# A block-causal attention and gMLP kernel on one core: from an order kept for TensorE alone to one order for every engine

## The chip, the cores and the metric

The kernel runs on one core of one Trainium2 chip. The metric is the device time of one execution in microseconds (us); before the change the median of three runs is 747.5 us (747.38 to 748.92). Five engines work side by side, each through its own list of instructions in a fixed order: PE (TensorE: matmuls, with weight loads as PEld), DVE (VectorE), ACT (ScalarE), POOL (GpSimd) and SP (SyncE, which here only issues DMAs). An instruction waits at the head of its engine's list until the semaphores it needs have been raised.

## What is computed

```python
# q, k, v: (8, 8, 576, 64); block = 64
scores = scale * np.matmul(q, k.transpose(0, 1, 3, 2))
scores = np.where(block_i >= block_j, scores, -1e9)
attn = softmax(scores)                      # max, exp, sum, divide
x = np.matmul(attn, v)  -> (8, 576, 512)    # heads side by side
h = np.maximum(x @ w_in, 0.0)               # 512 -> 1024
u, v = h[..., :512], h[..., 512:]
v_n = (v - mean(v)) / np.sqrt(var(v) + 1e-6)
v_s = np.einsum('ts,bsd->btd', w_spatial, v_n) + b_spatial[None, :, None]
out = (u * v_s) @ w_out                     # 512 -> 512
```

The large matmuls of the second half are done in float32r, each operand split into a high part and a rest (hi, lo), three products for one.

## The kernel before

A batch has 8 heads, worked as four **pairs** (pr 0 to 3) of two heads. Batch 0 has a start of its own, in which scores are transposed on TensorE and the weights are split in the background. From batch 1 on, a loop takes one pair after another (32 pairs in all, 28 of them in this loop), and into each pair's attention it weaves a quarter of the gMLP of the batch before.

For one pair, in the source's order:

- `scores_8`: the last 64 rows of both heads (tile **p8**, 128 x 576): two matmuls into two PSUM banks, a DVE pass that scales, masks and takes the row maximum (L476), Exp on ACT with the row sums (L483), sum and reciprocal on DVE (L491, L494), the scaling of p8 by the reciprocal on POOL (L497).
- one gMLP group, if the loop's credit allows (`group`).
- `scores_run`: the eight matmuls of the other rows into six banks, **p3** first (512 columns, one tile for each head), then p2, then p1 with p0; for each the same DVE pass, Exp, sum, scaling.
- `av_pair` of the pair *before*: the products with V into two banks, then `x_evac`: ACT casts the bank into x (L395), DVE subtracts for the rest (L396).
- `turn_blocks`: DVE transposes p in 32 x 32 blocks into the buffer pb (L556 to L558 for p8, L563 and L565 for the others), and `regroup` moves pb into ptt by eight DMAs (L574), for the next pair's `av_pair`. Three calls of these stand behind each gMLP group.

Six PSUM banks are used in a ring, ten to a pair: the first bank of `av_pair` is the one from which DVE reads the first head's p3, the second that of the second head's p3. Two more banks, ps_m, go round among the gMLP groups. A group's matmuls start when what was two groups earlier has been read out of its bank.

The groups of a batch's gMLP: v groups (mv; five, of 128 rows and the **tail** of 64), u groups (mu; eight), spatial groups (ms; eight), output groups (mo; eight). A v group has four stages: matmuls and read-out into vr (L623; for the tail L634, L635, L636); statistics (L640, L641); the reciprocal root by Ln and Exp on ACT (L643, L644) with four small DVE steps (L645 to L657); normalising and splitting on ACT (L662, L668) and POOL (L669). Stage 1 is emitted with the group, and each later group that is emitted moves all groups behind it one stage on (`issue`). An ms group is read out by a multiplication on DVE (u, L720), then cast (gh, L723) and subtracted (gl, L724). Its matmuls need all four full v groups' splits (vh, vl) and the tail's.

What sets the order: `mm` chains every matmul of the loop to the one before it, so PE follows the source. On DVE, ACT, POOL and SP a compile-time scheduler with a model of its own sets the order; it is free to put a ready instruction ahead of one that stands earlier in the source. At run time every engine's list is fixed.

Of the kernel before, what the change touches and what calls it, by code (L numbers as in the profile page):

```python
# [55 lines left out]
def kernel(  # L56
# [171 lines left out]
    last = [None]  # L228

    def mm(out, lhsT, rhs, start, stop):  # L230
        ins = nc.tensor.matmul(out, lhsT, rhs, start=start, stop=stop).ins  # L231
        if last[0] is not None:
            tc.add_manual_dep(
                ins, last[0].name,
                mybir.DependencyInfo(mybir.DependencyClass.NoSync, mybir.DependencyReason.DATA),
                reason="order",
            )
            last[0] = ins
        elif ordered:
            last[0] = ins  # L240

    ordered = []
# [32 lines left out]
    def scores(b, pr, i):  # L275
# [8 lines left out]
        if hd < 2:  # L284
# [5 lines left out]
            mm(ps[:, :n], raw[js, qs], raw[js, :n], True, True)  # L290
# [5 lines left out]
        else:  # L296
            n = S
            for z in range(2):
# [3 lines left out]
                mm(ps[:, :HT], raw[:, Q8:], raw[:, zs], True, True)  # L302
# [166 lines left out]
    def soft(st, t, hd, p, parts):  # L469
# [17 lines left out]
    def normalise(st, tiles):  # L487
# [13 lines left out]
    def scores_8(b, pr):  # L501
        raw = raws[(b, pr)]
        st = stats[(b, pr)] = st_p.tile([P, 32], F32, tag="sst", name=f"sst_{b}_{pr}", bufs=3)
        parts = []
        for z in range(2):
            ps = bank(f"s8_{b}_{pr}_{z}")
            mm(ps[:, :HT], raw[:, Q8:], raw[:, z * HT:(z + 1) * HT], True, True)
            parts.append(ps[:, :HT])
        soft(st, 8, 0, p8[:, :S], parts)
        normalise(st, [(8, 0, p8[:, :S])])  # L510

    def scores_run(b, pr):

# [3 lines left out]
        for t in (3, 2, 1, 0):  # L517
            for hd in range(2):
# [59 lines left out]
    def av_pair(b, pr):  # L578
        ptt = ptts.pop((b, pr))
        vt = vts.pop((b, pr))  # L580
        for z in range(2):
            av = bank(f"av_{b}_{pr}_{z}")
            to = av[:, :HT].rearrange("p (a q) -> p a q", a=2)
            for c in range(5):
                for j in range(2):
# [4 lines left out]
                        ptt[:, 2 * z:2 * z + 2, at:at + C_N[c]], c == 0, c == 4,  # L590
                    )
            x_evac(b, pr, av[:, :HT], lambda x, z=z: x[:, z * HT:(z + 1) * HT], HT)
        tail_evac(b, pr)


    def moe(b):
# [155 lines left out]
        order = "vuvuvuvuvuuuu" if b else "v" * 5 + "u" * 8  # L752
# [73 lines left out]
    ordered.append(True)  # L826
    queue = moe(0)
    credit = 0.0

    behind = []  # L830

    def issue(f):
# [6 lines left out]
        behind.append(gen)  # L839

    def group():
        nonlocal credit
        if queue and credit > 0.0:
            t, f = queue.pop(0)
            credit -= t
            issue(f)
            return True
        return False

    for g in range(NPAIR, len(pairs)):  # L850
        b, pr = pairs[g]
        credit += G_PAIR
        rest = []
        for hd in range(2):
            for t in (3, 2, 1, 0):
                rest.append(lambda t=t, hd=hd: turn_blocks(b, pr, t, hd))
            rest.append(lambda hd=hd: regroup(b, pr, hd))
        rest.insert(0, lambda: turn_blocks(b, pr, 8, 0))
# [92 lines left out]
```

## Time and profile before

| what | value |
|---|---|
| median of 3 runs | 747.5 us (747.38 to 748.92) |
| the profiled execution: its time, its span | 749.12 us, 747.3 us |
| granted TensorE clock, mean | 0.993 |
| busy in the span: PE, PEld, DVE, ACT, POOL | 93%, 78%, 62%, 51%, 37% |
| PE waiting for DVE's u (L720) before mo, in all | 19.9 us |
| ACT and POOL waiting for what DVE gives (the longest three kinds) | 107.4, 101.5 and 50.1 us |

From batch 2 on the profile repeats itself every 87.3 us, six times; PE is busy for 81.8 us of each. Names: s are score matmuls, p probabilities, sst their sums and maxima, av the products with V, mv, mu, ms, mo the gMLP's banks, vr and st a v group and its statistics. A row of the timeline has the start (us), the duration, engine, line, operation, output and inputs, partitions x elements, a count, and in brackets the idle time just before with the one who ended it.

### The profile page before, as it was taken

What the parts mean: (1) busy time and instruction counts of PE and PEld (TensorE: products, weight loads), DVE (VectorE), ACT (ScalarE), POOL (GpSimd) and SP (SyncE); (2) the same over time, 40 slices, a digit from 0 to 9 for tenths busy, and PEclk for the clock granted to TensorE, in tenths of its full rate; (3) what the DMA queues carried; (4) which work ended last, traced back from release to release, by engine and by line L of the source; (5) the groups of instructions that cost most, each with busy time, mean ns of one, the idle gap of its engine ahead of it and who ended that gap; (6) DMA issues with size and microseconds to landing.
All of it is one profiled execution on the core that took longest, in us unless ns stands there. A gap on an engine that the chain in (4) does not pass through costs nothing.

```text
span 747.3 us, 14409 instructions
## 1 busy us (share of the span) xinstructions
PE 691.7 (93%) x4864; PEld 583.6 (78%) x4864; DVE 464.9 (62%) x1755; ACT 383.8 (51%) x1088; POOL 276.4 (37%) x428
## 2 busy tenths in 40 slices
PE   9999787999999999999999999999999999999998
PEld 6545576977888877887788778888778877888897
DVE  5985686466666675557864666666755578543521
ACT  5866654545544564446644455444644466442532
POOL 4775455232434224233342324342242334422121
PEclk9999899999999999999999999999999999999999
DMA  6444553664544634656246645446346562344001
GB/s 211 145 142 143 150 142 107 159 178 96 140 111 129 186 102 100 168 149 163 68 124 156 174 103 139 107 130 177 106 103 172 142 170 65 94 121 120 1 16 48
DMA packets 53660, 94.42 MB, mean 126 GB/s; under 512 B 5970, under 2 KB 43346, under 8 KB 53588
## 3 DMA queue, kind: packets, MB, share of 16 engines
q1 hardware_dynamic: 53588, 93.52, 46.5%
q8 instruction: 38, 0.62, 0.3%
q14 instruction: 34, 0.28, 0.1%
HBM read 38.18 MB, written 9.44 MB: 64 GB/s over the span
## 4 chain that ended last, share of the span: by engine, by line
DVE 39%; PE 25%; ACT 16%; POOL 8%; issue 6%; DMA 3%; SPq 3%; POOLq 0%; DVEq 0%; ACTq 0%
PE mo L231 12%; DVE pb L563 9%; DVE p L476 8%; ACT p L483 7%; PE ms L231 6%; POOL p L497 4%; DVE st L640 3%; PE s L231 3%; ACT vr L662 3%; SPq L574 2%; DVE pb L556 2%; POOL vl L669 2%; PE mv L231 2%; DVE sst L491 1%; DVE vr L636 1%
## 5 line engine op out<-in xcount | busy, mean ns | idle before, releaser
L497 POOL TENSOR_SCALAR p<-p,sst 128x384 f32<-128x384 f32 (+4 forms) x252 | 136.2, 557 | 203.3 <-DVE sst L494 101.5
L483 ACT ACTIVATE p<-p,sst 128x384 f32<-128x384 f32 (+4 forms) x252 | 145.0, 577 | 47.6 <-DVE sst L476 44.6
L476 DVE CUSTOM_DVE_ANT_0 p<-s,mask 128x384 f32<-128x384 f32 (+4 forms) x252 | 113.9, 470 | 38.8 <-PE s L231 38.4
L231 PE MATMUL s<-raw 64*128 64x256 f32 (+4 forms) x640 | 127.6, 446 | 2.3 <-DVE nmax L291 1.8
L231 PE MATMUL mu<-x,wi_hi 128*128 128x288 f32 x512 | 113.2, 300 | 8.9 <-ACT u L694 8.9
L231 PEld LDWEIGHTS s<-raw 64*128 64x128 f32 (+1 forms) x640 | 73.6, 191 | 41.0 <-issue 23.3
L231 PE MATMUL mv<-wi_hi,x 128*128 128x512 f32 x256 | 90.2, 414 | 12.5 <-DVE vr L635 9.9
L563 DVE STREAM_TRANSPOSE pb<-p 128x384 f32<-128x384 f32 (+2 forms) x224 | 96.2, 452 | 5.6 <-POOL p L497 4.4
L231 PEld LDWEIGHTS mu<-x,wi_hi 128*128 128x128 f32 x512 | 85.4, 188 | 12.6 <-ACT u L694 10.5
L720 DVE TENSOR_TENSOR u<-ms,u 128x288 f32<-128x288 f32 x64 | 28.2, 441 | 100.3 <-PE ms L231 100.2
L231 PE MATMUL av<-ptt,v 128*64 128x32 f32 (+4 forms) x1120 | 86.8, 306 | 2.3 <-DVE sst L476 2.1
L231 PEld LDWEIGHTS av<-ptt,v 128*64 128x64 f32 x1120 | 77.0, 137 | 13.5 <-DVE sst L476 4.6
L723 ACT CAST gh<-u 128x288 fp32r<-128x288 f32 x64 | 27.6, 432 | 113.2 <-DVE u L720 107.4
L231 PE MATMUL ms<-ws_hi,vh 128*128 128x288 f32 x256 | 80.8, 316 | 3.6 <-ACT u L694 3.5
L669 POOL TENSOR_TENSOR vl<-vr,vh 128x512 fp32r<-128x512 f32 x32 | 41.2, 1288 | 102.8 <-ACT vh L668 102.7
L231 PE MATMUL ms<-ws_hi,vl 128*128 128x288 f32 x256 | 76.2, 298 | 1.0 <-POOL vl L669 0.3
L724 POOL TENSOR_TENSOR gl<-u,gh 128x288 fp32r<-128x288 f32 x48 | 38.4, 801 | 100.5 <-ACT gh L723 100.5
L231 PE MATMUL mo<-gh,wo_hi 128*128 128x288 f32 x256 | 56.9, 303 | 19.9 <-DVE u L720 19.9
L231 PE MATMUL ms<-ws_lo,vh 128*128 128x288 f32 x256 | 75.3, 294 | 0.0
L231 PEld LDWEIGHTS mv<-wi_hi,x 128*128 128x128 f32 x256 | 49.2, 192 | 28.6 <-DVE vr L635 11.9
L231 PE MATMUL mu<-x,wi_lo 128*128 128x288 f32 x256 | 69.8, 295 | 0.0
L745 ACT COPY o<-mo 128x288 f32<-128x288 f32 x64 | 25.5, 399 | 70.9 <-PE mo L231 62.6
(121 smaller groups left out, 1296.0 us busy)
## 6 DMA issues: line engine op xcount, KB each, us to landing
ptt<-pb SPq DMA_DIRECT2D x224, 200.0 KB, 4.0
raw<-qk SPq DMA_DIRECT2D x31, 608.0 KB, 3.8
v<-v SPq DMA_DIRECT2D x32, 320.0 KB, 3.0
outT<-o SPq DMA_DIRECT2D x64, 144.0 KB, 3.3
rwi<-w_in SPq DMA_DIRECT2D x8, 512.0 KB, 3.5
rwo<-w_out SPq DMA_DIRECT2D x4, 512.0 KB, 4.2
rws<-w_spT SPq DMA_DIRECT2D x4, 288.0 KB, 2.7
rwt<-w_spT SPq DMA_DIRECT2D x2, 144.0 KB, 4.8
```

The lines of the kernel that those rows point to most:

```text
L231: ins = nc.tensor.matmul(out, lhsT, rhs, start=start, stop=stop).ins
L476: nc.vector.tensor_tensor_reduce(out=p[:, at:at + n], in0=ps, in1=mk, scale=-0.125, scalar=BIG if m == 0 else st[:, k:k + 1], op0=ALU.add, ...
L483: nc.scalar.activation(p, p, AF.Exp, bias=mx, scale=-1.0, accum_out=st[:, 10 + k:11 + k])
L497: nc.gpsimd.tensor_scalar(out=p, in0=p, scalar1=st[:, k:k + 1], scalar2=1.0, op0=ALU.mult, op1=ALU.mult)
L563: nc.vector.transpose(to(hd * XH + 32 * t, [[P, m], *dims] if m > 1 else dims), p[:, :m * P])
L640: nc.vector.bn_stats(out=st[:m, 0:6], in_=vr[:m, :])
L662: nc.scalar.activation(vr[:m, :], vr[:m, :], AF.Identity, bias=st[:m, 13:14], scale=st[:m, 12:13])
L669: nc.gpsimd.tensor_tensor(out=vl, in0=vr, in1=vh.bitcast(F32), op=ALU.subtract)
L720: nc.vector.tensor_tensor(out=uz, in0=ps[:, :HT], in1=uz, op=ALU.mult)
L723: nc.scalar.copy(gh[:, dc, :], uz)
L724: (nc.vector if dc == ND - 1 else nc.gpsimd).tensor_tensor(out=gl[:, dc, :], in0=uz, in1=gh[:, dc, :].bitcast(F32), op=ALU.subtract)
L745: nc.scalar.copy(o, ps[:, :HT])
```

## The change

1. `mm` becomes a plain matmul. A new function `in_order` chains every instruction traced since its last call to the one before it *on the same engine*, for PE, DVE, ACT, POOL and SP. From batch 1's first pair on (batches counted from 0) all engines follow the source. `pass_over` leaves out what `step_background` emits: weight preparation, still in the scheduler's hands.
2. The source's order is written anew. p8's transposes stand right behind its scaling in `scores_8`. In `scores_run` the sum and reciprocal of a pair of tiles stand behind the DVE passes of the next pair of tiles, and p3's first transposes before the last of these. `av_pair` yields after each half, and transposes stand between the read-outs; one gMLP group stands behind the first head's p2, the others behind the last transposes.
3. The buffer vr has three places in place of two.
4. Batch 0's gMLP starts v v v u v u v u ..., with the tail third, in place of five v groups and then eight u groups.

No instruction is added or removed; PE's order is the same but for batch 0's gMLP.

```diff
-        f = ff_p.tile([P, 512], F32, tag="vr", name=f"f{name}", bufs=2)[:, :n]
+        f = ff_p.tile([P, 512], F32, tag="vr", name=f"f{name}", bufs=3)[:, :n]
...
+    def in_order():
+
+        new = traced.instructions[seen[0]:]
+        seen[0] += len(new)
+        for i in new:
+            if i.engine in last:
+                tc.add_manual_dep(
+                    i, last[i.engine].name,
...
+                )
+            last[i.engine] = i
+
+    mm = nc.tensor.matmul
...
-        soft(st, 8, 0, p8[:, :S], parts)
-        normalise(st, [(8, 0, p8[:, :S])])
+        top(st, 8, 0, p8[:, :S], parts)
+        norm(st, [(8, 0, p8[:, :S])])
+        turn_blocks(b, pr, 8, 0)
...
-            normalise(st, tiles)
+            if due:
+                norm(st, due)
+            due = tiles
+        turn_blocks(b, pr, 3, 0)
+        norm(st, due)
...
-            vr = ff_p.tile([P, DH], F32, tag="vr", name=f"vr_{b}_{c}", bufs=2)
+            vr = ff_p.tile([P, DH], F32, tag="vr", name=f"vr_{b}_{c}", bufs=3)
...
-        order = "vuvuvuvuvuuuu" if b else "v" * 5 + "u" * 8
+        order = "vuvuvuvuvuuuu" if b else "vvvuvuvuuuuuu"
...
         scores_8(b, pr)
+        in_order()
         group()
         scores_run(b, pr)
-        if g > NPAIR:
-            av_pair(*pairs[g - 1])
-            if pr == 0:
-                queue += moe(b - 1)
-        n = max(n, g * NT)
+        av = av_pair(*pairs[g - 1]) if g > NPAIR else iter([])
+        next(av, None)
+        turn_blocks(b, pr, 3, 1)
+        next(av, None)
+        next(av, None)
+        turn_blocks(b, pr, 2, 0)
+        in_order()
+        if g > NPAIR and pr == 0:
+            queue += moe(b - 1)
+        group()
+        turn_blocks(b, pr, 1, 0)
+        turn_blocks(b, pr, 0, 0)
+        regroup(b, pr, 0)
+        turn_blocks(b, pr, 2, 1)
+        turn_blocks(b, pr, 1, 1)
+        turn_blocks(b, pr, 0, 1)
+        regroup(b, pr, 1)
+        in_order()
         while group():
-            step_background(n)
-            n += 1
-            for f in rest[:3]:
-                f()
-            del rest[:3]
-        for f in rest:
-            f()
+            pass
```

How this moves instructions is shown at three places of batch 3, which stand for batches 2 to 7. The names carry batch, pair, head and a serial number; rows with `128x1` behind an `ISA` row are that pass's read-out of the maxima.

**DVE at pair 0, from p8's passes on; before:**

```order
L476 ISA p8_96,sst_3_0_2867<-s8_3_0_1_2870,mask_98,sst_3_0_2867 128x288
L476 ISA sst_3_0_2867 128x1
L476 ISA p3_3_0_0_2892,sst_3_0_2867<-s3_3_0_0_2878,mask_98 128x512
L476 ISA sst_3_0_2867 128x1
L491 TENSOR_SCALAR sst_3_0_2867<-sst_3_0_2867 128x1
L494 RECIPROCAL sst_3_0_2867<-sst_3_0_2867 128x1
L476 ISA p3_3_0_1_2895,sst_3_0_2867<-s3_3_0_1_2880,mask_98 128x512
L476 ISA sst_3_0_2867 128x1
L476 ISA p2_3_0_0_2902,sst_3_0_2867<-s2_3_0_0_2882,mask_98 128x384
L476 ISA sst_3_0_2867 128x1
L556 STREAM_TRANSPOSE pb_3_0_2972<-p8_96 128x3x8x16
```

**and in the changed kernel:**

```order
L484 ISA p8_96,sst_3_0_2867<-s8_3_0_1_2870,mask_98,sst_3_0_2867 128x288
L484 ISA sst_3_0_2867 128x1
L499 TENSOR_SCALAR sst_3_0_2867<-sst_3_0_2867 128x1
L502 RECIPROCAL sst_3_0_2867<-sst_3_0_2867 128x1
L574 STREAM_TRANSPOSE pb_3_0_2878<-p8_96 128x3x8x16
L575 STREAM_TRANSPOSE pb_3_0_2878<-p8_96 128x8x16
L576 STREAM_TRANSPOSE pb_3_0_2878<-p8_96 128x8x16
L484 ISA p3_3_0_0_2896,sst_3_0_2867<-s3_3_0_0_2882,mask_98 128x512
```

The first p3 pass, which frees `av_pair`'s first bank, stood right behind p8's passes; now it stands behind p8's sum, reciprocal and all three p8 transposes, and the first of these waits for POOL's scaling.

**ACT from the tail's read-out (mv_2_4) to p8's Exp of pair 1; before:**

```order
L662 ACTIVATE vr_2_1_3004<-vr_2_1_3004,st_2_1_3005 128x512
L634 COPY vr_2_4_3056<-mv_2_4_3055 64x512
L668 CAST vh_2_1_3090<-vr_2_1_3004 128x512
L694 ACTIVATE u_2_2992<-mu_2_0_2_3075 128x288
L643 ACTIVATE st_2_4_3057<-st_2_4_3057,eps_113 64x1
L644 ACTIVATE st_2_4_3057<-st_2_4_3057 64x1
L662 ACTIVATE vr_2_4_3056<-vr_2_4_3056,st_2_4_3057 64x512
L623 ACTIVATE vr_2_2_3097<-mv_2_2_3096 128x512
L675 CAST vs_a_123<-vr_2_4_3056 64x512
L483 ACTIVATE p8_96,sst_3_1_3122<-p8_96,sst_3_1_3122 128x576
```

**and in the changed kernel:**

```order
L655 COPY vr_2_4_3056<-mv_2_4_3055 64x512
L664 ACTIVATE st_2_1_3014<-st_2_1_3014,eps_113 128x1
L665 ACTIVATE st_2_1_3014<-st_2_1_3014 128x1
L715 ACTIVATE u_2_3008<-mu_2_0_2_3075 128x288
L683 ACTIVATE vr_2_1_3013<-vr_2_1_3013,st_2_1_3014 128x512
L689 CAST vh_2_1_3090<-vr_2_1_3013 128x512
L644 ACTIVATE vr_2_2_3097<-mv_2_2_3096 128x512
L664 ACTIVATE st_2_4_3057<-st_2_4_3057,eps_113 64x1
L665 ACTIVATE st_2_4_3057<-st_2_4_3057 64x1
L491 ACTIVATE p8_96,sst_3_1_3122<-p8_96,sst_3_1_3122 128x576
```

The tail's Ln and Exp (st_2_4), for which DVE's small steps wait, stood ahead of the next v group's read-out (vr_2_2); now they stand behind v group 1's normalising and cast and behind that read-out.

**ACT from the last v group's Exp (st_2_3) to the first gh; before:**

```order
L694 ACTIVATE u_2_2992<-mu_2_1_0_3261 128x288
L644 ACTIVATE st_2_3_3234<-st_2_3_3234 128x1
L662 ACTIVATE vr_2_3_3233<-vr_2_3_3233,st_2_3_3234 128x512
L694 ACTIVATE u_2_2992<-mu_2_1_1_3289 128x288
L668 CAST vh_2_3_3328<-vr_2_3_3233 128x512
L694 ACTIVATE u_2_2992<-mu_2_1_2_3313 128x288
```

**and in the changed kernel:**

```order
L715 ACTIVATE u_2_3008<-mu_2_1_1_3298 128x288
L664 ACTIVATE st_2_3_3243<-st_2_3_3243,eps_113 128x1
L665 ACTIVATE st_2_3_3243<-st_2_3_3243 128x1
L715 ACTIVATE u_2_3008<-mu_2_1_2_3318 128x288
L683 ACTIVATE vr_2_3_3242<-vr_2_3_3242,st_2_3_3243 128x512
L689 CAST vh_2_3_3333<-vr_2_3_3242 128x512
```

The last v group's normalising and cast stood ahead of the read-out of the last u group before the ms groups (mu_2_1_2); now they stand behind it.

More of the change, by code (lines that the diff above doesn't have):

```diff
@@ L225, in load_pair, with pass_over @@
         raws[(b, pr)] = raw
[L228 to L242, printed above, removed]
+    traced = nc.cur_bb.bb
+    last = {}
+    seen = [0]
+    def pass_over():
+        seen[0] = len(traced.instructions)
+    def in_order():
[5 more added lines that the diff above has]
+                    i, last[i.engine].name,
+                    mybir.DependencyInfo(
+                        mybir.DependencyClass.NoSync, mybir.DependencyReason.DATA
+                    ),
+                    reason="order",
+                )
+            last[i.engine] = i
+    mm = nc.tensor.matmul
     vts = {}
@@ L289, in scores @@
             raw = raws[(b, pr)]
-            mm(ps[:, :n], raw[js, qs], raw[js, :n], True, True)
+            mm(ps[:, :n], raw[js, qs], raw[js, :n], start=True, stop=True)
             nc.vector.tensor_tensor_reduce(
@@ L301, in scores @@
                 raw = raws[(b, pr)]
-                mm(ps[:, :HT], raw[:, Q8:], raw[:, zs], True, True)
+                mm(ps[:, :HT], raw[:, Q8:], raw[:, zs], start=True, stop=True)
                 nc.vector.tensor_tensor_reduce(
@@ L467, with top @@
              (1, 0): 4, (0, 0): 5, (1, 1): 6, (0, 1): 7, (8, 0): 8}
-    def soft(st, t, hd, p, parts):
+    def top(st, t, hd, p, parts):
         k = PLACE[(t, hd)]
@@ L485, in soft, with norm @@
         )
-    def normalise(st, tiles):
+    def norm(st, tiles):
         k0 = PLACE[tiles[0][:2]]
@@ L506, in scores_8 @@
             ps = bank(f"s8_{b}_{pr}_{z}")
-            mm(ps[:, :HT], raw[:, Q8:], raw[:, z * HT:(z + 1) * HT], True, True)
+            mm(ps[:, :HT], raw[:, Q8:], raw[:, z * HT:(z + 1) * HT], start=True, stop=True)
             parts.append(ps[:, :HT])
-        soft(st, 8, 0, p8[:, :S], parts)
-        normalise(st, [(8, 0, p8[:, :S])])
+        top(st, 8, 0, p8[:, :S], parts)
+        norm(st, [(8, 0, p8[:, :S])])
+        turn_blocks(b, pr, 8, 0)
     def scores_run(b, pr):
@@ L525, in scores_run @@
                         ps[(0, hd)] = bk[:, n:n + P]
-                mm(ps[(t, hd)], raw[js, S + t * P:S + (t + 1) * P], raw[js, :n], True, True)
+                mm(
+                    ps[(t, hd)], raw[js, S + t * P:S + (t + 1) * P], raw[js, :n],
+                    start=True, stop=True,
+                )
+        due = None
         for ts in ((3,), (2,), (1, 0)):
@@ L534, in scores_run @@
                     p_of[(b, pr, t, hd)] = p[:, at:at + n]
-                    soft(st, t, hd, p[:, at:at + n], [ps[(t, hd)]])
+                    top(st, t, hd, p[:, at:at + n], [ps[(t, hd)]])
                     tiles.append((t, hd, p[:, at:at + n]))
                     at += n
-            normalise(st, tiles)
+            if due:
[3 more added lines that the diff above has]
+        norm(st, due)
     pbs = {}
@@ L589, in av_pair @@
                         to[js, :, PA - C_N[c]:], vt[:, c, js],
-                        ptt[:, 2 * z:2 * z + 2, at:at + C_N[c]], c == 0, c == 4,
+                        ptt[:, 2 * z:2 * z + 2, at:at + C_N[c]],
+                        start=(c == 0), stop=(c == 4),
                     )
             x_evac(b, pr, av[:, :HT], lambda x, z=z: x[:, z * HT:(z + 1) * HT], HT)
+            yield
         tail_evac(b, pr)
+        yield
     def moe(b):
@@ L822 @@
         n += 1
-    ordered.append(True)
     queue = moe(0)
@@ L839, in issue @@
         behind.append(gen)
+        in_order()
     def group():
-        nonlocal credit
+        nonlocal credit, n
         if queue and credit > 0.0:
@@ L846, in group @@
             issue(f)
+            step_background(n)
+            pass_over()
+            n += 1
             return True
         return False
+    pass_over()
     for g in range(NPAIR, len(pairs)):
         b, pr = pairs[g]
+        n = max(n, g * NT)
         credit += G_PAIR
[L853 to L858, printed above, removed]
         scores_8(b, pr)
+        in_order()
         group()
         scores_run(b, pr)
-        if g > NPAIR:
-            av_pair(*pairs[g - 1])
-            if pr == 0:
-                queue += moe(b - 1)
-        n = max(n, g * NT)
-        while group():
-            step_background(n)
-            n += 1
-            for f in rest[:3]:
-                f()
-            del rest[:3]
-        for f in rest:
-            f()
+        av = av_pair(*pairs[g - 1]) if g > NPAIR else iter([])
[15 more added lines that the diff above has]
+        regroup(b, pr, 1)
+        in_order()
+        while group():
+            pass
         if g + 1 < len(pairs):
@@ L878 @@
             load_pair(*pairs[g + 2])
+        in_order()
     while queue:
         issue(queue.pop(0)[1])
-    av_pair(*pairs[-1])
+    run(av_pair(*pairs[-1]))
     for _, f in moe(B - 1):
@@ L884 @@
     for e in behind:
-        for _ in e:
-            pass
+        run(e)
 def tokens():
```

## The prediction

> **What bounds the kernel now.** I read the page first, then busy times by stretches, then whom PE waits for, then the timeline of one batch.
>
> ```profile
> PE 691.7 (93%) x4864; PEld 583.6 (78%) x4864; DVE 464.9 (62%) x1755; ACT 383.8 (51%) x1088; POOL 276.4 (37%) x428
> ...
> 65.00:130.00 65.00, 54.05 (x355) 44.20 (x351) 47.35 (x173) 35.81 (x100) 34.16 (x44) 0.95 0.49 137
> ...
> 217.40:304.70 87.30, 81.78 (x600) 70.88 (x600) 56.05 (x217) 44.90 (x129) 30.47 (x51) 1.00 0.51 134
> ...
> 653.90:747.30 93.40, 86.16 (x614) 79.29 (x613) 32.14 (x102) 33.90 (x87) 18.86 (x27) 1.00 0.23 61
> ```
>
> The columns of the last three are the stretch, its length, busy time and count of PE, PEld, DVE, ACT, POOL, granted clock, DMA share, GB/s. PE is the bound: 81.78 of 87.30 us in a steady batch. No engine gets less work by this change, and PE's order stays, so it can only act through PE's idle time: 5.5 us in each of six steady batches, 11 in the stretch 65 to 130, 7 at the end; in all 747.3 - 691.7 = 55.6. What ends PE's waits in the steady batch:
>
> ```profile
> PE mo L231 <- DVE u L720: 2.8, 2, 1.4
> PE mu L231 <- ACT u L694: 1.3, 1, 1.3
> PE mv L231 <- DVE vr L635: 0.9, 1, 0.9
> ```
>
> All three are read-outs that stand late in DVE's or ACT's list: banks, not data. The same can happen to av: its first bank is the one from which DVE reads p3, and a row of batch 1 shows PE held by it.
>
> ```profile
> 122.01 3.10 PE L231 MATMUL av<-ptt,v 128*64 128x288 f32 x40 [0.92 <-DVE sst L476]
> ```
>
> So I walk each place where PE waits through one batch (247.25 to 334.43, the same as the others) with the new lists and the old durations. "+" is how much later PE passes a point than in the rows; lines are the old kernel's.
>
> **Pair 0: p8's wait in front of p3.** At a batch's first pair no gMLP group stands between `scores_8` and av.
>
> ```profile
> 249.16 0.78 ACT L483 ACTIVATE p<-p,sst 128x576 f32<-128x576 f32 x1 [1.27 <-DVE sst L476]
> 249.47 0.69 DVE L476 CUSTOM_DVE_ANT_0 p<-s,mask 128x512 f32<-128x512 f32 x1 [0.40 <-PE s L231]
> 250.60 0.74 POOL L497 TENSOR_SCALAR p<-p,sst 128x576 f32<-128x576 f32 x1 [8.91 <-DVE sst L494]
> ...
> 250.66 3.03 PE L231 MATMUL av<-ptt,v 128*64 128x288 f32 x40
> 255.45 0.49 PE L231 MATMUL mv<-wi_hi,x 128*128 128x512 f32 x1 [0.17 <-ACT x L395]
> ```
>
> Before, DVE read p3 at 249.47 while ACT and POOL worked on p8, and av began the moment PE was free. Now DVE stands idle until POOL has p8, at 251.34. Three transposes follow: 0.50 + 0.23 + 0.23, by starts in the rows of pair 2 below, so p3 is read from 252.4 to 253.0 and av starts at 253.1, **+2.4**. Eight Exps follow p3's first pass, 4.5 us by the rows at 297.73 and 301.83, then the x cast, 0.35, for which mv's fourth pair of products waits: 258.1 for 255.45, **+2.65**.
>
> ```profile
> 297.73 0.72 ACT L483 ACTIVATE p<-p,sst 128x512 f32<-128x512 f32 x1 [1.39 <-DVE sst L476]
> 301.83 0.39 ACT L483 ACTIVATE p<-p,sst 128x128 f32<-128x128 f32 x1
> ```
>
> **The tail's bank: a gain.** PE waited at 267.51 for the tail's read-out, which now stands ahead of v group 1's small steps, and vr's third place takes POOL out of its way. At +2.65 PE ends the tail at 267.5; ACT copies at once (0.6, taken as L623's below), DVE adds (0.7, as L640's), so the bank is free at 269.0, just before PE comes at 269.1: **+1.6**.
>
> ```profile
> 267.51 0.50 PE L231 MATMUL mv<-wi_hi,x 128*128 128x512 f32 x1 [0.93 <-DVE vr L635]
> 267.50 1.41 DVE L636 TENSOR_SCALAR vr<-vr 64x512 f32<-64x512 f32 x1
> 271.10 0.44 DVE L476 CUSTOM_DVE_ANT_0 p<-s,mask 128x288 f32<-128x288 f32 x1
> 274.68 0.68 DVE L476 CUSTOM_DVE_ANT_0 p<-s,mask 128x512 f32<-128x512 f32 x1
> 275.42 3.09 PE L231 MATMUL av<-ptt,v 128*64 128x288 f32 x40
> ```
>
> **Pair 1: the largest term.** Mean durations in ns, in the view that groups instructions, behind the bar and the busy time:
>
> ```profile
> L668 ACT CAST vh<-vr 128x512 fp32r<-128x512 f32 x32 | 19.7, 617 | 0.3
> L623 ACT ACTIVATE vr<-mv 128x512 f32<-128x512 f32 x32 | 18.9, 589 | 13.6 <-PE mv L231 12.2 <-POOL vl L669 1.4
> L640 DVE BATCH_NORM_STATS2 st<-vr 128x6 f32<-128x512 f32 x32 | 21.6, 677 | 20.9 <-ACT vr L623 20.7
> L643 ACT ACTIVATE st<-st,eps 128x1 f32<-128x1 f32 x32 | 9.4, 294 | 37.9 <-DVE st L641 34.9 <-DVE sst L494 3.0
> ```
>
> DVE goes on from 268.85: L636, 1.41; v group 1's small steps, 0.95, at 271.2. Only now can ACT normalise that group (0.82, row 286.95 below), cast it (0.62), read out v group 2 (0.59), and then do the tail's Ln and Exp (0.5), for which DVE's next small step waits: until 273.7. Three small steps, 0.75, and p8's passes start at 274.4, where they were at 271.10. From there: passes 0.95, Exp 0.95, sum and reciprocal 0.4, POOL 0.85, transposes 1.0, the tail's cast, subtraction and v group 2's statistics (0.35 + 0.7 + 0.85, behind the transposes now), p3's pass 0.6: av at 281.2. PE has finished its scores at 277.0 and is idle for 4.2; av was at 275.42, **+5.8**. Bounds: were p8's passes as early as PE allows (272.0), the stall would be 1.7 and this +3.3; ACT's hand-overs could add 1.
>
> **The last v group before ms.**
>
> ```profile
> 286.07 0.40 PE L231 MATMUL mu<-x,wi_hi 128*128 128x288 f32 x1 [1.31 <-ACT u L694]
> 286.95 0.81 ACT L662 ACTIVATE vr<-vr,st 128x512 f32<-128x512 f32 x1 [0.84 <-DVE st L657]
> 288.65 1.28 POOL L669 TENSOR_TENSOR vl<-vr,vh 128x512 fp32r<-128x512 f32 x1 [4.04 <-ACT vh L668]
> 289.99 0.40 PE L231 MATMUL ms<-ws_hi,vl 128*128 128x288 f32 x1
> ```
>
> The wait at 286.07 goes, about 1.6 with the refill. But the normalising that stood at 286.95, ahead of the last u read-out, now follows it: after mu_2_1_2's last matmul come read-out 0.4, normalising 0.75, cast 0.6, POOL 1.3, 3.1 with hand-overs, and PE has only 11 matmuls (1.5 us) before it needs vl. DVE's statistics of this group, behind five transposes, add 0.7. The one about pays for the other: the first ms group ends at 296.15 for 290.49, **+5.65**.
>
> **Pairs 2 and 3.**
>
> ```profile
> 295.44 0.44 DVE L720 TENSOR_TENSOR u<-ms,u 128x288 f32<-128x288 f32 x1
> 296.47 0.58 DVE L556 STREAM_TRANSPOSE pb<-p 128x384 f32<-128x384 f32 x1 [0.59 <-POOL p L497]
> 296.97 0.65 DVE L476 CUSTOM_DVE_ANT_0 p<-s,mask 128x512 f32<-128x512 f32 x1
> 297.56 0.31 DVE L557 STREAM_TRANSPOSE pb<-p 128x128 f32<-128x128 f32 x1
> 297.79 0.65 DVE L476 CUSTOM_DVE_ANT_0 p<-s,mask 128x512 f32<-128x512 f32 x1
> 297.69 3.09 PE L231 MATMUL av<-ptt,v 128*64 128x288 f32 x40
> 305.81 0.63 PE L231 MATMUL mo<-gh,wo_hi 128*128 128x288 f32 x3 [1.37 <-DVE u L720]
> ```
>
> The two small transposes (0.23 each, from 297.56 to 297.79) and u, which filled the wait for POOL at 295.44, now lie between L556 and p3: 0.83, av +0.75. In pair 2 the last ms group's u passes five transposes (2.0 us), the gain meant at 305.81; but p3's delay, and the sum of p1, which now waits for all Exps with the x read-outs and p3's transposes behind it (0.5 idle), take that back: u ends 0.25 later, **+5.9** at mo. In pair 3 the third u is as early as before, but the fourth now follows all transposes (before, two were left), so gh and gl for mo's last products come 0.9 late: **+6.8** a batch.
>
> **What should cost nothing.** On SP the loads of the next K and Q now follow a pair's regroup and outT, at the end of its section and no longer behind its scores.
>
> ```profile
> raw<-qk SPq DMA_DIRECT2D x31, 608.0 KB, 3.8
> ```
>
> They are needed a whole pair later (87.3 / 4 = 21.8 us), so the slack of some 18 us hides 3.8; without it each would cost up to 3.8 a pair. p8's transposes must not write pb before the last regroup has left it: in pair 0 some 11 us lie between.
>
> **The sum.** Six steady batches (1 of 7 has its own case, below): 6 x 6.8 = 41. The first stretch: tail third and u between take about 4 us out of waits (3.9 at 83.72, below), then DVE has weight preparation, the tail and statistics in front of pair 1's p8 and p3, some 6 us late at av, of which later idle time gives some back: +3, bounds -3 and +8. The last gMLP alone: the vl wait, +1, bounds 0 and 2. Then the clock:
>
> ```profile
> 80.00:85.00 5.00, 1.28 (x3) 1.09 (x4) 2.62 (x7) 1.96 (x4) 2.86 (x3) 0.71 0.92 209
> 85.00:90.00 5.00, 5.00 (x18) 4.05 (x18) 3.26 (x13) 2.80 (x7) 0.67 (x1) 0.60 0.73 212
> ...
> 83.72 0.79 PE L231 MATMUL mv<-wi_hi,x 128*128 128x512 f32 x1 [3.90 <-DVE vr L635]
> 88.99 0.29 PE L231 MATMUL mu<-x,wi_hi 128*128 128x288 f32 x1
> ```
>
> After the one PE gap of 3.9 us the granted clock was 0.60, and a v group took 5.27 (83.72 to 88.99) where one takes about 2.85. My 4.2-us gap stands in six batches: nothing, or 2.4 each, 14. With one such gap in the trace and a little doubt that mine is that long, I take 3. Together 41 + 3 + 1 + 3 = 48. The profiled execution took 749.1 (span 747.3 and 1.8 around it), 1.6 above the median: about 797 by it, **795** by the median.
>
> The Trainium skill, "TensorE: Matmul & The Clock Gate", section "Part 1: The HAM clock gate (the "warmup" mystery)", says that the array's clock is halved after an idle window of about 3.4 us, and that the window runs freely. The rows at 80 to 90 agree in kind (0.60 to 0.71 after 3.9 us). By the rule a 4.2-us gap holds a whole window in about one batch of four, an estimate from that page; it would put the clock's term at about 4 for my 3.
>
> **The rivals.**
>
> - *Pair 1 is mostly hidden* (0.15): the small steps run ahead of my walk and its stall is 1.7. Then a batch costs 6.8 - 2.5 = 4.3, no clock term: 6 x 4.3 + 1 + 0 = 27, 774. For it: I added hand-overs by hand; against it: the lists leave no other order.
> - *The clock drops each time* (0.07): 14 for 3, 806, and to 816 if batch 1 is at its bound.
> - *The read-outs win* (0.08, the other side): p8's latency is covered since p3's passes are not what av ends up waiting for. Then the gains stand alone: 0.9 at the tail, 1.3 at mu, 1.4 at mo, six times 3.6 = 22, and 4 in batch 1: 721. It decides from the point where DVE's three transposes end before PE's scores do. Against it: in pair 0 POOL's row ends at 251.34, after 250.66.
> - *No difference* (0.03): gains and stalls cancel, or waits move within PE's 5.5 idle us: 748.
>
> The forecast itself has 0.67, its own range 779 to 809. A difference under 0.2% (1.5 us) can't be told from none here. Faster 0.09, same 0.03, slower 0.88. The range 764 to 814 leaves out the last two rivals and the far ends.
>
> **What would show it.** Right: PE's waits name av <- DVE sst L484 four times a batch, about 2.4, 4.2, 0.8, 0.8; ms waits for POOL vl (L690) near 1; mv <- DVE vr is gone; the period is near 94 with PE busy 82. The clock falls below 1.00 after pair 1's gap or not. Wrong: av starts with no wait in pair 0, or the wait at mo shrinks with the period at 85 or less.

## The result and the profile after

The changed kernel takes 845.9 us (median of 4 runs, 842.75 to 847.99) where the kernel before takes 747.4 beside it: a ratio of 1.131 (95% interval 1.127 to 1.135). Slower was forecast, at 795; the loss is 98 us and not 48, outside the range. The profiled execution has a span of 842.5 us. Below are the engines' busy times from its page, then whom PE waits for (after the colon the total in us, how often, the longest wait), then one steady batch (266.67 to 369.05, columns as in the prediction):

```profile
PE 724.4 (86%) x4864; PEld 616.2 (73%) x4864; DVE 483.8 (57%) x1755; ACT 386.2 (46%) x1088; POOL 277.7 (33%) x428
```

```profile
PE av L606 <- DVE sst L484: 45.7, 22, 5.7
PE mo L760 <- DVE u L741: 21.6, 14, 2.5
PE mo L760 <- ACT gh L744: 17.0, 15, 2.1
PE av L606 <- DMA raw<-qk: 8.3, 5, 2.2
PE ms L734 <- ACT vh L689: 7.7, 7, 1.2
PE ms L734 <- POOL vl L690: 5.7, 7, 0.8
```

```profile
266.67:369.05 102.38, 87.44 (x602) 76.36 (x601) 58.79 (x216) 45.00 (x129) 30.56 (x50) 0.93 0.43 114
```

The number of matmuls is the same, yet PE is busy for 724.4 us and not 691.7: the granted clock fell (0.947 on average, for 0.993). Idle time went from 55.6 us to 842.5 - 724.4 = 118.1. So the span's growth of 95.2 is 62.5 of waiting and 32.7 of slower matmuls. A steady batch shows the same split: it takes 102.4 us for 87.3, with 87.4 busy for 81.8 and 14.9 idle for 5.5. The wait put down to the transfer of K and Q is no new one: it lasts 2.24 us in pair 0 of three batches and 0.77 in pair 3 of two, as long as the wait for DVE at the same place in the other batches (2.24 or 2.25, and 0.76 or 0.77), so the transfer was only the last thing to end.

The stalls at av, DVE and PE in the timeline, pair 0 and then pair 1:

```profile
269.67 0.17 DVE L502 RECIPROCAL sst<-sst 128x1 f32<-128x1 f32 x1
270.79 0.58 DVE L574 STREAM_TRANSPOSE pb<-p 128x384 f32<-128x384 f32 x1 [0.95 <-POOL p L505]
271.68 0.65 DVE L484 CUSTOM_DVE_ANT_0 p<-s,mask 128x512 f32<-128x512 f32 x1
272.40 4.77 PE L606 MATMUL av<-ptt,v 128*64 128x288 f32 x40 [2.25 <-DVE sst L484]
...
297.50 0.58 DVE L574 STREAM_TRANSPOSE pb<-p 128x384 f32<-128x384 f32 x1 [0.95 <-POOL p L505]
298.39 0.38 DVE L695 CAST vs_b<-vr 64x512 fp32r<-64x512 f32 x1
299.50 0.69 DVE L661 BATCH_NORM_STATS2 st<-vr 128x6 f32<-128x512 f32 x1
300.32 0.66 DVE L484 CUSTOM_DVE_ANT_0 p<-s,mask 128x512 f32<-128x512 f32 x1
301.05 5.83 PE L606 MATMUL av<-ptt,v 128*64 128x288 f32 x40 [3.81 <-DVE sst L484]
```

DVE stands at p8's transposes until POOL has scaled p8, then does them, in pair 1 also the tail's cast and the next statistics, and only then reads p3, whose bank av needs. That is the walk of the prediction. What it had not seen are the durations: av takes 4.77 and 5.83 us in place of 3.03 and 3.09, because the clock was halved behind each stall.

### The profile page after: what moved, and what is told of

It is laid out like the page before. It is cut to its first block, busy times and chain, and to the rows that moved or that the text cites. A ratio compares the mean times of both kernels' runs of the same rounds, so it can differ in the third digit from the quotient of the medians.

```text
span 842.5 us, 14409 instructions
## 1 busy us (share of the span) xinstructions
PE 724.4 (86%) x4864; PEld 616.2 (73%) x4864; DVE 483.8 (57%) x1755; ACT 386.2 (46%) x1088; POOL 277.7 (33%) x428
## 5 line engine op out<-in xcount | busy, mean ns | idle before, releaser
L505 POOL TENSOR_SCALAR p<-p,sst 128x384 f32<-128x384 f32 (+4 forms) x252 | 137.5, 560 | 312.4 <-DVE sst L502 272.9
L606 PE MATMUL av<-ptt,v 128*64 128x32 f32 (+4 forms) x1120 | 113.1, 366 | 53.9 <-DVE sst L484 45.7
L606 PEld LDWEIGHTS av<-ptt,v 128*64 128x64 f32 x1120 | 100.1, 168 | 69.0 <-DVE sst L484 59.1
L484 DVE CUSTOM_DVE_ANT_0 p<-s,mask 128x384 f32<-128x384 f32 (+4 forms) x252 | 108.1, 478 | 44.8 <-PE s L515 42.7
L710 PE MATMUL mu<-x,wi_hi 128*128 128x288 f32 x512 | 111.1, 298 | 1.4 <-ACT vr L644 1.4
L760 PE MATMUL mo<-gh,wo_hi 128*128 128x288 f32 x256 | 63.9, 323 | 38.6 <-DVE u L741 21.6
L581 DVE STREAM_TRANSPOSE pb<-p 128x384 f32<-128x384 f32 (+1 forms) x224 | 91.4, 448 | 0.0
L760 PEld LDWEIGHTS mo<-gh,wo_hi 128*128 128x128 f32 x256 | 46.1, 208 | 45.0 <-issue 24.5
L536 PE MATMUL s<-raw 64*128 64x512 f32 (+1 forms) x448 | 68.6, 443 | 0.0
L536 PEld LDWEIGHTS s<-raw 64*128 64x128 f32 x448 | 41.2, 186 | 28.3 <-issue 19.3
L760 PE MATMUL mo<-gl,wo_hi 128*128 128x288 f32 x256 | 61.0, 322 | 0.0
L639 PEld LDWEIGHTS mv<-wi_hi,x 128*128 128x128 f32 x256 | 49.3, 193 | 14.9 <-ACT vr L644 2.4
```

The lines of the kernel that those rows point to most:

```text
L484: nc.vector.tensor_tensor_reduce(out=p[:, at:at + n], in0=ps, in1=mk, scale=-0.125, scalar=BIG if m == 0 else st[:, k:k + 1], op0=ALU.add, ...
L505: nc.gpsimd.tensor_scalar(out=p, in0=p, scalar1=st[:, k:k + 1], scalar2=1.0, op0=ALU.mult, op1=ALU.mult)
L581: nc.vector.transpose(to(hd * XH + 32 * t, [[P, m], *dims] if m > 1 else dims), p[:, :m * P])
L606: mm(to[js, :, PA - C_N[c]:], vt[:, c, js], ptt[:, 2 * z:2 * z + 2, at:at + C_N[c]], start=(c == 0), stop=(c == 4),)
L639: mm(ps, xs[k][:, j, cs], w[:, k, DH:], start=(n == 0), stop=(n == 3 * NC - 1),)
L710: mm(ps[:, :HT], w[:, k, ds], xs[k][:, j, zs], start=(n == 0), stop=(n == 3 * NC - 1),)
```

## What was left out: the clock and mo

The clock first, in stretches of 1 us (granted clock third from the end), then of 3.41 us; first among the busy times is PE's:

```profile
272.00:273.00 1.00, 0.60 (x5) 0.51 (x7) 1.00 (x5) 0.56 (x1) 0.00 (x0) 0.95 0.81 329
276.00:277.00 1.00, 1.00 (x17) 1.00 (x13) 0.83 (x4) 1.00 (x6) 0.72 (x2) 0.85 0.00 0
300.00:301.00 1.00, 0.00 (x0) 0.00 (x0) 0.97 (x5) 0.00 (x0) 0.00 (x0) 0.60 0.00 0
307.00:308.00 1.00, 1.00 (x5) 0.82 (x6) 0.65 (x2) 0.31 (x1) 0.75 (x3) 0.99 0.00 0
337.00:338.00 1.00, 1.00 (x7) 0.94 (x8) 1.00 (x5) 0.18 (x1) 0.76 (x1) 0.87 0.00 0
```

```profile
156.84:160.25 3.41, 1.34 (x9) 1.29 (x10) 1.67 (x5) 0.76 (x2) 0.81 (x2) 1.00 0.60 89
160.25:163.66 3.41, 3.41 (x16) 3.41 (x15) 0.00 (x0) 0.40 (x1) 0.00 (x0) 0.50 0.89 236
...
170.49:173.91 3.42, 1.46 (x21) 1.40 (x21) 3.07 (x11) 1.42 (x4) 0.32 (x1) 1.00 0.36 149
173.91:177.32 3.41, 3.24 (x34) 2.53 (x30) 3.10 (x17) 3.41 (x16) 2.35 (x4) 1.00 0.01 2
```

In these traces the clock is either 1.00 or 0.50, so a mean of 0.95 over 1 us says that it fell 0.1 us before the end: at 272.9. Likewise it rose at 276.3, fell at 300.2, rose at 307.0 and fell at 337.74. From 272.9, these lie 3.4, 27.3, 34.1 and 64.8 us on: 1, 8, 10 and 19 times 3.413. So the clock is set anew every 3.413 us on a grid that runs on whatever the kernel does; it stays halved for whole windows of 3.413 us, and this batch has four of them (272.9, two from 300.2, 337.74), which take away up to half of 13.7 us, 6.8, of PE's work. In the second fence, a window with 1.34 us of PE work is followed by a halved one, and a window with 1.46 is not. In thirteen of the fifteen traces the clock falls while PE still has work (in e6 and e7, below, only after its last matmul). In these thirteen the least idle time in a whole window that a halving followed is 1.41 us (e4), and the most in one that was not followed by it 1.96 (e3). A gap of 2.24 us was enough where it lay in one window. A window that is already halved needs less: it was followed by another halved one with as little as 0.49 us idle (e11), and by the full clock with 0.70 at most (e2). So pair 1's stall, which ends 0.85 us into the window from 300.2, costs two windows.

The Trainium skill, "TensorE: Matmul & The Clock Gate", section "Part 1: The HAM clock gate (the "warmup" mystery)", says the window lasts 3413 ns and runs freely: the traces agree to the digit. It says too that the clock drops after an idle window; here 1.34 us of work in the window did not prevent it, and between 1.41 and 1.96 us of idle time, 41 to 57% of a window, both outcomes occur. What decides between them the runs do not show.

Now mo: rows of ACT, DVE and PE in order of time, from pair 2 and then from pair 3:

```profile
333.34 0.70 ACT L403 CAST x<-av 128x288 fp32r<-128x288 f32 x2 [1.88 <-PE mu L710]
333.77 0.46 DVE L404 TENSOR_TENSOR x<-av,x 128x288 fp32r<-128x288 f32 x1 [1.55 <-ACT x L403]
335.65 0.42 DVE L741 TENSOR_TENSOR u<-ms,u 128x288 f32<-128x288 f32 x1
336.22 0.50 PE L760 MATMUL mo<-gh,wo_hi 128*128 128x288 f32 x2 [2.52 <-DVE u L741]
...
359.98 1.60 DVE L581 STREAM_TRANSPOSE pb<-p 128x256 f32<-128x256 f32 x5
361.50 0.42 DVE L741 TENSOR_TENSOR u<-ms,u 128x288 f32<-128x288 f32 x1
362.78 0.40 PE L760 MATMUL mo<-gh,wo_hi 128*128 128x288 f32 x1 [2.06 <-ACT gh L744]
```

In pair 2, x's cast waits until 333.34 for the last u group of the batch before (mu). There are five x buffers (L83); the one that pair 2 writes is the one of that batch's first pair, which this mu still reads. DVE's x waits for the cast, and u stands behind x, where before x stood behind u. So mo waits 2.52 us, and the clock halves once more. In pair 3 the fourth u stands behind the last five transposes, and mo waits 0.55 and 2.06.

## The experiments

Times are medians (of two executions for e1 to e4, e8 and e12, of four to ten for the others), the kernel before beside them between 746.8 and 749.4. Comments in the code of e5 and e13 are added here, and one line of e1 is broken in two.

| run | us | ratio to before (95%) |
|---|---|---|
| e1 stalls at av filled with PE work | 848.0 | 1.135 (1.132 to 1.138) |
| e2 p8's transposes behind p3 | 810.6 | 1.085 (1.082 to 1.088) |
| e3 u ahead of x | 821.3 | 1.099 (1.096 to 1.103) |
| e12 e1 and e3 together | 813.2 | 1.089 (1.079 to 1.098) |
| e4 DVE free | 775.2 | 1.038 (1.032 to 1.043) |
| e8 ACT free | 805.2 | 1.076 (1.072 to 1.079) |
| e6 only PE in order | 743.7 | 0.994 (0.992 to 0.996) |
| e7 vr's third place and batch 0's order alone | 741.1 | 0.991 (0.988 to 0.993) |
| e5 fixed order, stalls undone | 770.2 | 1.029 (1.026 to 1.033) |
| e9 fixed order, better | 753.4 | 1.007 (1.005 to 1.010) |
| e10 e9 with p8's transposes early | 788.8 | 1.055 (1.051 to 1.059) |
| e11 e9 with x ahead of u | 771.5 | 1.032 (1.028 to 1.036) |
| e13 fixed order, mended | 722.4 | 0.964 (0.962 to 0.966) |

**e1: is the clock a cost of its own?** Behind the last score matmul of pairs 0 and 1:

```diff
-        due = None
+        due = [mm(ps[(0, 1)], raw[64:, S:S + P], raw[64:, :P], start=True, stop=True)
+               for _ in range({0: 9, 1: 16}.get(pr, 0))] and None
```

> The changed kernel with PE's two longest stalls filled: behind the last score matmul of a batch's pair 0 that 64 x 128 matmul is repeated 9 times, of pair 1 16 times, into the same bank, which DVE reads later anyway (about 1.9 and 3.4 us of PE work where PE stood idle for 2.2 and 3.8). Nothing that waits is moved. Theory (the clock is a cost of its own): the granted clock no longer falls in these two places, where it was halved for 3.4 and 6.8 us a batch, so 1.7 + 3.4 us of lost array time a batch come back, less what later waits swallow: 812 to 824 us, mean clock from 0.947 to 0.97 or more, while the stalls at av stay as they are. Rival (the slow clock lies in time that the waits set anyway): 840 to 850 us.

The first row below is pair 0's av, the others are two neighbouring windows behind mo in pair 2:

```profile
278.11 3.10 PE L606 MATMUL av<-ptt,v 128*64 128x288 f32 x40 [0.23 <-DVE sst L484]
```

```profile
337.73:341.14 3.41, 1.56 (x9) 1.30 (x10) 2.91 (x10) 1.07 (x3) 1.11 (x2) 1.00 0.00 0
341.14:344.55 3.41, 3.41 (x16) 3.41 (x16) 0.57 (x3) 0.40 (x1) 0.00 (x0) 0.50 0.66 110
```

The theory's number was wrong. The rival's number was right, but its reason is not shown, since the clock was not repaired: it did stay whole at both av (3.10 us), but it now fell at other places: at 320.66 behind the waits at ms, at 341.14 behind mo in pair 2 (second fence), and for two windows behind mo in pair 3. That is again four halved windows a batch, and the period is again 102.4 us. So what a batch loses to the clock hangs on all the idle time in its windows and on where the grid falls; taking two idle stretches away did not give back their share. Both kernels' period is 30.0 windows of 3.413 us. Others settle on whole windows too (e11 below at 92.2 us, 27.0; e9 drifts from 26.2 to 26.0), and some don't (e3 stays between 28.9 and 29.6 but for one batch, e4 between 26.8 and 27.3). It looks as if batches can lock to the grid, since a batch that ends late moves an idle stretch into or out of a window; that was not tested.

**e12: the same with e3's edit,** which takes mo's long gap of pair 2 away.

> The changed kernel with the two edits of earlier runs together: the stalls of pairs 0 and 1 filled with repeated score matmuls, and u ahead of x in pairs 2 and 3. Theory (the clock is halved for a whole window of 3.41 us whenever PE was idle for about 1.5 to 2 us of the window before, wherever that is): what is left are the waits of 1.2 and 0.8 us close together at ms and about 2 to 2.8 us at mo, so one or two halved windows a batch stay: 803 to 822 us, mean clock 0.96 to 0.975. Rival (only the two long stalls at av halve it): clock above 0.985 and 797 us or less.

813.2 us, within the window theory's range; its two executions took 818.2 us at a mean clock of 0.962 and 808.2 at 0.975. The 8 us to e3 alone are no more than the distance between these two.

**e2: p8's transposes behind p3's passes.**

```diff
         norm(st, [(8, 0, p8[:, :S])])
-        turn_blocks(b, pr, 8, 0)
...
-            if due:
-                norm(st, due)
+            norm(st, due) if due else turn_blocks(b, pr, 8, 0)
```

> The changed kernel with p8's three transposes behind the two p3 passes in place of ahead of them; all else in the order of the source. Theory (DVE stands at p8's transposes for POOL while av's bank waits for p3): PE's wait for av goes in pairs 0, 2 and 3 (2.2, 0.8 and 0.8 us) and falls from 3.8 to about 1.9 in pair 1, where the tail's cast, subtraction and a v group's statistics still stand ahead of p3; the halved clock goes in pair 0 and mostly in pair 1. Some 8 to 10 us a batch: 780 to 797 us. Rival (the frozen lists of ACT, POOL and SP are the cost): above 820 us.

```profile
265.40 3.09 PE L606 MATMUL av<-ptt,v 128*64 128x288 f32 x40 [0.33 <-DVE sst L484]
292.32 3.09 PE L606 MATMUL av<-ptt,v 128*64 128x288 f32 x40 [2.79 <-DVE sst L484]
```

35 us less than the changed kernel, for the 49 to 66 expected: 810.6 lies between the theory's range and the rival's. Pair 0's stall is gone as said (0.33), but pair 1 keeps 2.79 for the 1.9 expected: p8's sum, the tail's cast, which waits for ACT, its subtraction and the statistics still stand ahead of p3.

**e3: u ahead of x in pairs 2 and 3** (av's read-outs emitted behind the next gMLP group).

> The changed kernel with the read-outs of av (x) in pairs 2 and 3 emitted behind the gmlp group that follows av, so that on DVE the multiplication u and on ACT gh stand ahead of x. PE's order is the same. Theory (in pair 2, x's cast waits for the u group that reads the old x, and u stands behind it on DVE): PE's wait for u at the first mo of pair 2 falls from 2.5 to 0.5 us or less and the halved clock behind it goes (1.7 us), pair 3 stays with its fourth u behind the transposes: 3 to 4.5 us a batch, 817 to 828 us. Rival (the transposes ahead of u are the cost, not x): the wait stays above 1.5 us and the time above 838.

24.6 us less, as the theory said. PE's wait of mo for u, 21.6 us in all, is gone from the view (the wait for gh rises from 17.0 to 22.1). So x ahead of u, with its own wait for the old x, was the cause in pair 2, and not the transposes.

**e4, e8, e6: which engine's order costs.** One line chooses the engines that are chained:

```diff
-            if i.engine in last:
+            if i.engine in last and i.engine in KEEP:
```

> The changed kernel with DVE alone left to the scheduler; PE, ACT, POOL and SP stay in the order of the source. Theory (what costs is DVE's order): the waits at av go, and u comes ahead of transposes again; ACT's own placements (the tail's Ln and Exp behind a v group's normalising, the last normalising behind u) leave 1 to 3 us a batch over the kernel before: 750 to 775 us. Rival (ACT's frozen list costs as much as DVE's): 790 us or more.

> The changed kernel with ACT alone left to the scheduler; PE, DVE, POOL and SP stay in the order of the source. Theory (DVE's order is most of the cost): 815 to 848 us, the waits at av nearly as they were. Rival (ACT's order is half of it): 790 us or less.

> The changed kernel with only PE in the order of the source and the scheduler free on DVE, ACT, POOL and SP, as in the kernel before; the rewritten source, vr's third place and batch 0's new order stay. Theory (the loss comes from the fixed lists): 742 to 757 us, PE's order being the old one but for batch 0. Rival (the rewritten source, p8's transposes and the delayed norms, costs also where the scheduler is free): 765 us or more.

With only PE chained the loss is gone (743.7): the rewritten source costs next to nothing where the scheduler is free (87.9 us a batch, for 87.2 in e7). ACT, POOL and SP in order add 32 us to that (e4, at the upper end of its theory), DVE, POOL and SP 62, all of them 102. DVE's order is the larger part, but ACT's is more than I expected: with ACT free, 805 lies between the rival's 790 and the theory's 815. The traces show where: with ACT free, mo's waits for u and gh fall from 38.6 us in all to 7.5 (10.0 more are then put down to other read-outs), while av's wait stays (53.2 us, for 45.7 and the 8.3 put down to K and Q). POOL's and SP's order alone were not tried.

```profile
PE av L606 <- DVE sst L484: 53.2, 27, 6.0
...
PE mo L760 <- DVE u L741: 3.8, 7, 0.6
PE mo L760 <- ACT gh L744: 3.7, 7, 0.5
```

**e7: vr's third place and batch 0's order alone,** in the kernel before.

> The kernel before with two parts of the change alone: vr with three places, and batch 0's gmlp as v v v u v u v u ... with the tail third. Theory: the first gmlp's 3.9-us wait and its clock loss shrink (up to 4 us), and the wait of mv for vr in each batch (0.9) may go: 738 to 747 us. Rival: no difference beyond 1.5 us.

```profile
75.53 0.50 PE L231 MATMUL mv<-wi_hi,x 128*128 128x512 f32 x1 [1.01 <-DVE vr L635]
```

The two small parts of the change are a gain of 7 us (0.9%), which the changed kernel has too. It comes from batch 0: the gap of 3.90 us at 83.72 is now one of 1.01, and the clock stays at 1.00. The steady batch is the same (87.2 for 87.3), so the third place is worth next to nothing there.

**e5, e9: a fixed order with other placements.** Every engine stays in the source's order. The core of the edit in e5, which e9 keeps with more conditions:

```diff
-        norm(st, [(8, 0, p8[:, :S])])
-        turn_blocks(b, pr, 8, 0)
...
+            norm(st, due) if due else (norm(st, [(8, 0, p8[:, :S])]), settle() if held else None)
+            ts == (2,) and turn_blocks(b, pr, 8, 0)
...
+            settle()          # the steps of earlier groups first, then the new group
+            next(gen)
```

> The changed kernel, still with every engine in the order of the source, but with the placements that the changed trace shows PE waiting on written differently: p8's sum and its POOL scaling behind the p3 passes and its transposes behind the p2 passes; the steps of earlier gmlp groups that a group inside the scores brings with it behind the p3 passes; the steps of earlier groups ahead of a new group's read-out everywhere else (the tail's Ln and Exp, the last normalising, gh); in pairs 2 and 3 both u of the second part ahead of x and of the last transposes. Theory (it is these places, not a fixed order as such): PE's waits at av, mo and ms fall to under 1 us each, no PE gap reaches 2 us, the clock stays at 1.00, and a steady batch takes 83 to 88 us: 720 to 755 us. Rival (a fixed order on all engines costs by itself, wherever things stand): 770 us or more.

The waits of av for DVE and of mo for u are gone from the view, yet at 770.2 us the time is at the rival's lower bound: a read-out that frees a bank now stood behind the steps that I had moved ahead of it. A mu behind the last v group waits 2.48 us for it, and the clock halves.

```profile
290.21 0.60 PE L710 MATMUL mu<-x,wi_hi 128*128 128x288 f32 x1 [2.48 <-ACT vr L644]
```

e9 puts most of these read-outs first again, and starts the order in batch 2:

> Every engine in the order of the source from batch 2 on (batch 1 left to the scheduler but for PE), with the placements of the run that undid the stalls, and what still waited there mended: in pair 1 the tail's cast, subtraction and the next statistics behind all DVE passes; the read-outs of v and u groups ahead of the normalising of earlier groups, but for the group behind the tail and the last u before ms, where the earlier steps come first; in pairs 2 and 3 gh and gl ahead of the last scaling, and the first head's transposes between the two u. Theory (a fixed order costs nothing where no read-out that frees a bank stands behind a wait): a steady batch takes 83 to 87 us, the clock stays at 1.00: 712 to 742 us. Rival (some cost belongs to a fixed order): 755 us or more.

```profile
283.83 0.40 PE L735 MATMUL ms<-ws_hi,vh 128*128 128x288 f32 x1 [2.41 <-ACT u L716]
287.21 0.61 PE L735 MATMUL ms<-ws_hi,vh 128*128 128x288 f32 x1 [1.91 <-ACT vh L690]
288.55 0.61 PE L735 MATMUL ms<-ws_hi,vl 128*128 128x288 f32 x1 [0.50 <-POOL vl L691]
```

Between the two theories' numbers, with 4.8 us of waits a batch left at one place: the last v group's chain runs behind transposes on DVE, the last u read-out behind its normalising.

**e10, e11: one placement of the change put back into e9.**

> The run beside it (best order) with one placement of the change alone: p8's sum, POOL scaling and three transposes ahead of the p3 passes. Theory: PE waits at av for DVE's p3 in all four pairs, 2 to 2.5 us in pair 0, 1.5 to 2.5 in pair 1 and 0.75 in pairs 2 and 3, and at some of the longer two the clock halves (1.7 each): 5.5 to 10 us a batch, 33 to 62 us over the best order. Rival (p8's latency matters only together with the other placements): under 15 us over it.

> The best order with one other placement of the change alone: in pairs 2 and 3 both read-outs of av (x) ahead of the u that mo waits for. Theory (x's cast waits in pair 2 for the last u group of the batch before, which still reads the old x): PE's wait at the first mo of pair 2 grows by 1 to 2.5 us, pair 3 by 0 to 1: 1 to 3.5 us a batch, 6 to 23 us over the best order. Rival: under 3 us over it.

```profile
251.01 4.77 PE L607 MATMUL av<-ptt,v 128*64 128x288 f32 x40 [2.90 <-DVE sst L484]
276.85 3.09 PE L607 MATMUL av<-ptt,v 128*64 128x288 f32 x40 [1.02 <-DVE sst L484]
...
305.03 3.10 PE L607 MATMUL av<-ptt,v 128*64 128x288 f32 x40 [0.74 <-DVE sst L484]
```

```profile
308.74 0.63 PE L761 MATMUL mo<-gh,wo_hi 128*128 128x288 f32 x3 [1.41 <-DVE u L742]
```

p8's sum, scaling and transposes early cost 35 us over e9, x ahead of u 18: both within the theory's range, each in an order that otherwise differs from the change. For p8 the waits at av are 2.90 us in pair 0, 1.02 in pair 1 (1.5 to 2.5 was expected) and 0.74 in pair 2, and the clock again halves behind the first (av 4.77).

**e13: the stall of e9 mended.** In pair 1 the tail's split goes ahead of the scores, and the last v group's chain ahead of the remaining transposes and of x:

```diff
+            group(alone=True)          # v group 3: matmuls and read-out
+            step(6)                    # v group 2: normalising, split
+            group(alone=True)          # u
+            step(8)                    # v group 3: statistics
+            turn_blocks(b, pr, 3, 1)
+            step(8)                    # Ln, Exp, small steps
+            group(alone=True)          # u
+            step(8)                    # normalising, split
+            group(alone=True)          # u
+            next(av)                   # x
```

> The best order with what still waited there mended, every engine still in the order of the source from batch 2 on: in pair 1 the tail's normalising and split ahead of the scores, the last v group's chain (statistics, Ln and Exp, small steps, normalising) ahead of the transposes and of x, its read-outs in the order in which PE needs the banks; in pair 0 the read-outs of av ahead of the last scores' Exps. Theory (a fixed order has no cost of its own, only what waits in it): PE's waits at ms fall from 2.4 + 1.9 + 0.5 to 1.5 us or less in all, no window holds 2 us of idle PE, the clock stays at 1.00 and a steady batch takes 82 to 85.5 us: 712 to 737 us, faster than the kernel before. Rival (a fixed order always loses what the scheduler's order gains): 745 us or more, with waits turned up elsewhere.

```profile
PE 683.3 (95%) x4864; PEld 575.6 (80%) x4864; DVE 469.4 (65%) x1755; ACT 387.6 (54%) x1088; POOL 279.4 (39%) x428
```

```profile
PE av L609 <- DMA ptt<-pb: 9.8, 12, 1.3
PE ms L737 <- POOL vl L693: 5.4, 7, 0.8
PE mo L763 <- POOL gl L748: 4.3, 6, 0.7
```

722.4 us, 3.6% faster than the kernel before, every engine in a fixed order from batch 2 on. Of this, 0.9% is what e7 shows for vr and batch 0; the rest, 2.7%, comes with the new order. A steady batch takes about 84 us. This settles what e5 and e9 left open: the order as such costs nothing that these runs show, only what waits in it. What is left are waits of av for the regroup's transfers and of ms and mo for POOL.

## Why the prediction was wrong, point by point

- **Pair 0** (+2.4 at av): right. The stall is 2.24, and av starts 5.73 us into the section for 3.41, +2.32. But the next step, mv waiting for x (+2.65), did not occur: av itself took 1.74 longer at the halved clock, so that x came in time.
- **The tail's bank:** the wait is gone, as said; PE is 2.4 us late there for 1.6.
- **Pair 1** (a stall of 4.2, av +5.8): right, 3.81 and +6.2 (34.38 into the batch for 28.17), with p8's chain as walked.
- **The first ms:** forecast +5.65, measured +9.1 (318.99 - 266.67 for 290.49 - 247.25). The waits are 1.2 and 0.8, near the walk; the rest is mostly the halved clock behind pair 1's stall, at which av takes 5.83 us for 3.09.
- **Pairs 2 and 3, the first failed step:** "In pair 2 the last ms group's u passes five transposes (2.0 us), the gain meant at 305.81". The stalls at av are as forecast (0.76 in both pairs), but this gain is not there: u also went behind x, and x behind the last mu, by the five x buffers. I listed what stood ahead of u on DVE, but not what the new neighbour waits for itself. Pair 3's fourth u cost 2.06 where I had 0.9. Waits at mo are 5.3 us a batch, where before they were 2.7. With this a batch's idle time grew by 9.4 us, for 6.8 forecast.
- **The clock, the second failed step and the larger:** "nothing, or 2.4 each, 14 ... I take 3." I tied it to one gap of 4.2 us a batch, by the one row where 3.9 us had been followed by it, and took 3 of the 14 although I called the doubt little. Gaps of 2.2 to 2.5 do it too, and from batch 3 on four windows of a batch were halved: PE's busy time grew by 5.7 us a batch, 32.7 in all, eleven times the term. The rows in the prediction could have shown it. A mean clock of 0.71 from 80 to 85 us, with a clock of 1.00 or 0.50, says that it fell at 82.1, when PE had been idle for 2.3 us and not for 3.9. It had also halved at 58.24, behind a window with 1.8 us idle. The rival that came nearest ("the clock drops each time") priced one gap as well, and its upper figure should be 811, 806 and 5 for batch 1, not 816. One row seemed to speak against it: a gap of 2.37 us that ends at 131.11 left the clock whole. But the grid has a line at 129.92, which leaves 1.2 us of it on either side.
- **What should cost nothing:** the loads of K and Q did not hold PE up beyond the waits for DVE at the same places.
- **The sum:** of the span's growth of 95.2 us, 48 were forecast. The waiting grew by 62.5 for the 45 of its terms (41 + 3 + 1), PE's busy time by 32.7 for 3: of the 47 missing, 30 are the clock and 17 the waits (2.6 in a steady batch). This splits the span into busy and idle time. Where a slower av only filled a wait to come, as in pair 0, a whole clock would have gained less, and no run kept the clock whole with the waits as they are. By place, the changed kernel is 9.2 us behind at batch 2's first av (172.45 for 163.21), for 5.4 forecast (3 and that stall); 85.6 come from there to the last av, 12.5 in batch 2 with two halved windows and 14.9 to 15.2 in each of batches 3 to 6 with four, where 6.8 was forecast; and 0.3 behind it, for 1.

## What to carry to other kernels

Before an order is frozen, go through every read-out that frees a bank and ask of each instruction newly ahead of it what that one waits for, on its own engine and on others, down to the buffer it writes; the frozen orders here lost by these chains, and gained (about 2.7% in e13) once they were gone. Where PE is the bound, price new idle time twice: its length, and up to 1.7 us, half of a window of 3.413 us, for each window that it leaves idle for 2 us or more; between 1.41 and 1.96 us it may or may not come. Filling some of several gaps gained nothing in e1, as the others halved the clock in their place.

## What the runs showed of the hardware

The granted clock changes only on a grid of 3.413 us that is fixed for a whole execution, in every trace that has more than one change. A halving lasts one to three whole windows; it followed windows with as little as 1.41 us of idle PE, and all those with 2.0 or more, and it went on through windows with as little as 0.49. PE's idle time is taken from matmul records whose ends are modelled, so these limits are approximate. Two kernels with stalls at different places (the changed one and e1) settled at the same period of 102.4 us, 30.0 windows, with four halved ones in each batch, and two more at 27.0 and 26.0 windows; why they settle there was not tested.
